# Gates of a gated linear recurrence in polar form by prefix sums, instead of products doubled level by level

## The chip, the cores and the metric

The kernel runs on one core of one Trainium2 chip. The metric is the device time of one execution in microseconds (us). TensorE (PE) multiplies matrices, VectorE (DVE), ScalarE (ACT) and GpSimd (POOL) work on elements, and SyncE (SP) issues transfers. In the profile a float32 matmul stands as two records, each with a weight load (PEld).

## The reference

An attention block with a complex gate per channel is followed by a feed-forward block (FFN). There are 4 batches, 8 heads, 768 tokens and 48 channels per head; the FFN has 3072 tokens, width 384 and inner width 1024. All inputs are float32 except the four FFN weights, which are float64.

```python
a_re = rand * 0.1 + 0.85 ; a_im = randn * 0.1
mag = sqrt(a_re * a_re + a_im * a_im)
scale = minimum(mag, 0.999) / (mag + 1e-06)
for t in range(S):                       # S_re, S_im: 48 x 48 per head
    new_re = ar * S_re - ai * S_im       # ar, ai: a_re, a_im times scale, at t
    new_im = ar * S_im + ai * S_re
    S_re, S_im = new_re + outer(k[t], v[t]), new_im
    y[t] = q[t] @ S_re
x = y.transpose(0, 2, 1, 3).reshape(3072, 384)
out = (((x @ w1) * (x @ w2)) @ w3) @ w_out
```

## The kernel before

A unit is one batch and two heads (16 units); head g lies on partitions 64g to 64g+47, time on the free axis. Time is cut into six chunks of 128 tokens. Inside a chunk, the decay from token s to token t is a product of gates. It is built in seven levels n = 1, 2, 4 ... 64. At each level the buffers Q (q times gates) and K (k times gates) are multiplied in place, on VectorE, by the products X of the gates over half blocks (lines 209 to 218), and GpSimd makes the products of the next level from those of this one (lines 221 to 225). TensorE makes the scores of the pairs of tokens that part at this level: for n up to 16 in blocks of 32 tokens (lines 160 to 166), which VectorE takes over by mask into D (lines 170 and 177), and for n = 32 and 64 directly (lines 190 and 194). At the end of a unit K is transposed (line 237), kv sums are made (line 244), the state goes from chunk to chunk on VectorE (lines 250 and 253), and the outputs ys are summed from the scores A and the state (lines 263 and 266).

The gates are brought to their norm at the start of a unit (lines 130 to 141), among it a reciprocal on VectorE (line 135).

The FFN of a batch waits for all its heads: x is turned by transposes (line 282), then `ffn_ab` makes two products of 128 x 384 and multiplies them (lines 292 to 297), and `ffn_out` multiplies by the fused matrix w3 w_out (line 302). The FFN of batch b is dealt out between the levels of the units of batch b+1; the FFN of the last batch stands alone at the end. In batch 0 the weights take its place: `convert` (lines 326 to 338) turns float64 words to float32 in 36 pieces of up to 128 x 512, and `fuse` (line 349) makes w3 w_out.

The framework orders the instructions of each engine when the kernel is built, by its own model of costs; each engine then runs its list in order. Pools with one, two or three buffers decide when a tile can be written again.

## Time and profile before

| what | value |
|---|---|
| time, 3 runs | 1482.57, 1486.88 and 1487.62 us; median 1486.88 |
| span of the profiled execution, first to last instruction | 1493.7 us |
| mean granted TensorE clock | 0.754 |
| VectorE busy | 1175.4 us, 79% |
| TensorE busy | 1064.2 us, 71% |
| GpSimd busy | 562.4 us, 38% |
| ScalarE busy | 204.5 us, 14% |
| bytes moved | 48.85 MB, 33 GB/s |

The profiled execution's own time is known only as its span; the span is 6.8 us over the median of the runs, so whatever lies around it is smaller than the spread between executions. The clock is the share of full speed that TensorE was granted. In a row of the profile stand the line of the kernel, the engine, the operation, the tile written and the tiles read, the shape and the count; behind the bar the busy time in us, the mean of one in ns, and the idle time ahead of it with what ended it.

### The profile page before, as it was taken

The numbers are of one execution on the slowest core, as the hardware profiler recorded it, in microseconds if no ns is written. First come the engines' busy times: TensorE is split into PE (matmuls) and PEld (weight loads), VectorE is DVE, ScalarE is ACT, GpSimd is POOL, SyncE is SP. The second block draws the span as 40 slices with busy tenths as digits, with TensorE's granted clock in tenths as the row PEclk, the third lists the DMA queues.
The fourth block names the chain that finished last, engine by engine and source line by source line (L and its number), as shares of the span: only waits on it lengthen the run. The fifth ranks groups of instructions, "written<-read, shape, count | busy, mean of one in ns | idle before, by whom it ended". The sixth has DMA issues, their size and how long they took to land.

```text
span 1493.7 us, 42142 instructions
## 1 busy us (share of the span) xinstructions
PE 1064.2 (71%) x19304; PEld 755.5 (51%) x19304; DVE 1175.4 (79%) x1674; ACT 204.5 (14%) x362; POOL 562.4 (38%) x533
## 2 busy tenths in 40 slices
PE   0262767553276786969787968787798878787999
PEld 0252435342264564646565646465565555555755
DVE  9788989889877797888887878788877979796000
ACT  1010001010011111111211211120112020201111
POOL 5427226326218071616270534335431708080000
PEclk9985676755558686888769867877677778786899
DMA  3211222212110010101010100101010100000000
GB/s 101 57 56 47 78 69 60 78 52 61 45 31 25 11 33 13 46 3 41 21 38 3 33 21 18 30 9 45 14 34 10 39 21 10 2 7 12 2 16 16
DMA packets 35698, 48.85 MB, mean 33 GB/s; under 512 B 15552, under 2 KB 26816, under 8 KB 35520
## 3 DMA queue, kind: packets, MB, share of 16 engines
q1 hardware_dynamic: 35520, 46.15, 11.0%
q8 instruction: 151, 2.47, 0.7%
q14 instruction: 27, 0.22, 0.1%
HBM read 41.42 MB, written 4.72 MB: 31 GB/s over the span
## 4 chain that ended last, share of the span: by engine, by line
PE 46%; DVE 30%; issue 11%; POOL 11%; ACT 1%; DMA 0%; SPq 0%; POOLq 0%; DVEq 0%; ACTq 0%
PE m L292 14%; PE o L302 8%; PE sc L164 5%; DVE St L253 5%; DVE V L215 4%; DVE U L216 4%; DVE Q L218 4%; PE ys L266 3%; PE sc L190 3%; PE ys L263 3%; DVE K L218 3%; PE sc L166 3%; POOL f L336 3%; POOL X L224 2%; POOL XV L221 2%
## 5 line engine op out<-in xcount | busy, mean ns | idle before, releaser
L164 PE MATMUL sc<-Q,K 48*32 48x16 f32 x6144 | 147.3, 198 | 144.3 <-DVE Q L218 57.9
L164 PEld LDWEIGHTS sc<-Q,K 48*32 48x32 f32 x6144 | 132.3, 114 | 186.4 <-issue 152.5
L166 PE MATMUL sc<-Q,K 48*32 48x16 f32 x6144 | 142.1, 188 | 38.1 <-issue 35.9
L292 PE MATMUL m<-xT,w2s 128*128 128x384 f32 x384 | 164.2, 557 | 2.8 <-issue 2.3
L132 POOL TENSOR_TENSOR mag<-mag,den 128x768 f32<-128x768 f32 x16 | 29.0, 1811 | 364.3 <-ACT den L131 364.3
L190 PE MATMUL sc<-Q,K 48*32 48x32 f32 (+1 forms) x2304 | 78.0, 257 | 117.4 <-DVE K L218 116.1
L292 PE MATMUL m<-xT,w1s 128*128 128x384 f32 x384 | 159.5, 540 | 3.0 <-issue 3.0
L302 PE MATMUL o<-w3o,ab 128*128 128x384 f32 x384 | 158.9, 562 | 1.1 <-issue 1.1
L166 PEld LDWEIGHTS sc<-Q,K 48*32 48x32 f32 x6144 | 132.9, 122 | 49.2 <-issue 41.5
L266 PE MATMUL ys<-St,Q 48*128 48x48 f32 x640 | 135.8, 339 | 27.2 <-DVE St L253 25.9
L223 POOL TENSOR_TENSOR XV<-X 128x384 f32<-128x384 f32 (+6 forms) x112 | 85.8, 766 | 177.6 <-ACT X L139 177.6
L266 PEld LDWEIGHTS ys<-St,Q 48*128 48x128 f32 x640 | 111.0, 240 | 63.0 <-DVE St L253 31.0
L224 POOL TENSOR_TENSOR X<-X 128x1152 f32<-128x1152 f32 (+6 forms) x112 | 139.1, 1242 | 0.0
L225 POOL TENSOR_TENSOR X<-X,XV 128x1152 f32<-128x1152 f32 (+6 forms) x112 | 131.8, 1177 | 8.8
L218 DVE TENSOR_TENSOR Q<-U,V 128x384 f32<-128x384 f32 x224 | 126.7, 599 | 10.3 <-PE sc L166 9.3
L190 PEld LDWEIGHTS sc<-Q,K 48*32 48x32 f32 (+1 forms) x2304 | 69.8, 166 | 126.8 <-issue 120.0
L216 DVE TENSOR_TENSOR U<-Q,X 128x768 f32<-128x768 f32 x112 | 129.6, 1157 | 0.0
L221 POOL TENSOR_TENSOR XV<-X 128x768 f32<-128x768 f32 (+6 forms) x112 | 117.7, 1051 | 19.7 <-ACT X L139 12.4
L215 DVE TENSOR_TENSOR V<-Q,X 128x768 f32<-128x768 f32 x112 | 122.9, 1097 | 0.0
L297 DVE TENSOR_TENSOR ab<-m,a 128x384 f32<-128x384 f32 x64 | 35.4, 553 | 110.7 <-PE m L292 99.9
L336 POOL TENSOR_TENSOR f<-f,e 128x512 int32<-128x512 int32 (+1 forms) x36 | 51.8, 1438 | 157.1 <-DVE f L334 156.2
L263 PE MATMUL ys<-v,A 128*128 128x48 f32 x384 | 97.5, 362 | 14.1 <-ACT A L194 14.1
(71 smaller groups left out, 1706.2 us busy)
## 6 DMA issues: line engine op xcount, KB each, us to landing
raw<-in_w_dram SPq DMA_DIRECT2D x28, 512.0 KB, 3.6
v<-in_v_dram SPq DMA_DIRECT2D x16, 288.0 KB, 3.1
X<-in_a_re_dram SPq DMA_DIRECT2D x32, 144.0 KB, 2.9
X<-in_a_im_dram SPq DMA_DIRECT2D x32, 144.0 KB, 3.4
K<-in_k_dram SPq DMA_DIRECT2D x32, 144.0 KB, 2.7
Q<-in_q_dram SPq DMA_DIRECT2D x32, 144.0 KB, 3.6
out_dram<-ot SPq DMA_DIRECT2D x24, 192.0 KB, 1.9
raw<-in_w_out_dram SPq DMA_DIRECT2D x8, 384.0 KB, 3.1
```

Of the source, the lines that this page charges most:

```text
L164: nc.tensor.matmul(out=o, lhsT=K[ROWS[g], 0, t0:t0 + SB], rhs=qr[ROWS[g], 1, nb], start=True, stop=False)
L166: nc.tensor.matmul(out=o, lhsT=K[ROWS[g], 1, t0:t0 + SB], rhs=qr[ROWS[g], 0, nb], start=False, stop=True)
L190: nc.tensor.matmul(out=o, lhsT=K[ROWS[g], x, t0:t0 + n], rhs=Q[ROWS[g], 1 - x, t0 + n:t0 + 2 * n], start=(x == 0), stop=(x == 1))
L215: nc.vector.tensor_tensor(out=V, in0=Z, in1=wide(x[:, 0:2], 2), op=OP.mult)
L216: nc.vector.tensor_tensor(out=U, in0=Z, in1=wide(x[:, 2:3], 2), op=OP.mult)
L218: nc.vector.tensor_tensor(out=Z[:, y], in0=U[:, y], in1=V[:, 1 - y], op=OP.add)
L221: nc.gpsimd.tensor_tensor(out=XV[:, 0:2], in0=XR[:, 0:2], in1=XL[:, 2:3].to_broadcast([P, 2, nb]), op=OP.mult)
L224: nc.gpsimd.tensor_tensor(out=X2, in0=XL, in1=XR[:, 2:3].to_broadcast([P, 3, nb]), op=OP.mult)
L263: nc.tensor.matmul(out=o, lhsT=A[:, g, c], rhs=vt[:, c, g * D:(g + 1) * D], start=True, stop=(c == 0))
L266: nc.tensor.matmul(out=o, lhsT=Q[ROWS[g], 1 - x, c * C:(c + 1) * C], rhs=St[ROWS[g], c - 1, x], start=False, stop=(x == 1))
L292: nc.tensor.matmul(out=m, lhsT=w[:, f, j * P:(j + 1) * P], rhs=xT_t[b, h][:, f], start=(f == 0), stop=(f == KD - 1))
L302: nc.tensor.matmul(out=m, lhsT=ab_t[b, h][:, f, t * P:(t + 1) * P], rhs=w3o[:, f], start=(f == 0), stop=(f == KF - 1))
```

## The change

The kernel before becomes a function, `general`, that runs only where a flag, `good`, is zero at the end. Ahead of it stands a new path for gates with limits: the flag is set when no decay over a chunk is below e^-32, no angle is beyond 50, the real parts are within limits and no |a_im / a_re| is over 1.5 (`judge`). For the gates of the reference the logarithm of |a| is near -0.1, so that a chunk of 128 tokens comes to about -13, and the angle grows by steps of about 0.11.

In the new path a unit is half a batch (384 tokens, all 8 heads), with all 384 channels on 3 x 128 partitions; there are 8 units of three chunks. `gates` takes the logarithm of the magnitude and the arctangent, sums both along time with scans (lines 487 and 517), takes exponentials, sines and cosines, and multiplies q and k by them. So q is turned by its own angle and scaled by the decay since the start of the chunk, k by the inverse, and one product of 96 channels (real and imaginary part below each other) gives the scores of a head in a chunk. For that, the rows of a head are brought together in KL and QL by 40 transfers inside the chip's memory per unit (line 551). `scores` transposes the k parts (line 569), makes one product per head (line 574) and masks it (line 575). `outputs` writes y turned, as the FFN wants it, in blocks of 32 channels (lines 592 to 603), and carries the state T (kv on line 610, then VectorE on lines 614 to 617); GpSimd spreads v into V ahead of it (lines 438 to 440). `gates` of the next unit and the FFN of the unit before are interleaved with a unit's scores and outputs. `convert` needs three operations of VectorE instead of six, and two of ScalarE. The function `general` is as before except that it writes x with other channel positions and has no interleaving.

```diff
-def tile_gateloop__then__multiplicative_ffn_kernel(
+def general(ctx, tc, qt, kt, v, art, ait, w1s, w2s, w3o, ident, out):
...
+    def gates(u, split):
+        b, h = divmod(u, 2)
...
+        nc.scalar.preload_act_table_set("natural_log_exp_and_others")
+        for s in parts:
+            act(out=A[:, s], in_=re[:, s], func=AF.Ln)
+            act(out=r[:, s], in_=A[:, s], func=AF.Exp, scale=-1.0)
+        yield
+        for i, s in enumerate(parts):
+            nc.gpsimd.tensor_tensor(out=im[:, s], in0=im[:, s], in1=r[:, s], op=OP.mult)
+            act(out=Z[:, s], in_=re[:, s], func=AF.Relu, scale=-1.0, bias=LEAST, accum_out=st_low[:, 0, u, i:i + 1])
+            act(out=Z[:, s], in_=re[:, s], func=AF.Relu, bias=MOST, accum_out=st_low[:, 1, u, i:i + 1])
+        yield
+        for i, s in enumerate(parts):
+            nc.vector.tensor_tensor_reduce(out=Z[:, s], in0=im[:, s], in1=im[:, s], scale=1.0, scalar=0.0,
+                                           op0=OP.mult, op1=OP.max, accum_out=st_tan[:, u, i:i + 1])
+        yield
+        for s in parts:
+            act(out=Z[:, s], in_=Z[:, s], func=AF.Ln, bias=ONE)
+        yield
+        for s in parts:
+            stt(out=A[:, s], in0=Z[:, s], scalar=0.5, in1=A[:, s], op0=OP.mult, op1=OP.add)
+            act(out=Z[:, s], in_=A[:, s], func=AF.Exp, scale=-1.0, bias=EPS)
+        yield
+        for s in parts:
+            ts(out=A[:, s], in0=A[:, s], scalar1=LN_MAX, scalar2=None, op0=OP.min)
+        for s in parts:
+            for f in range(s.start, s.stop):
+                for c in range(UC):
+                    w = slice(c * C, (c + 1) * C)
+                    nc.vector.tensor_tensor_scan(out=r[:, f, w], data0=A[:, f, w], data1=Z[:, f, w], initial=0.0,
+                                                 op0=OP.add, op1=OP.subtract)
+        yield
+        for s in parts:
+            act(out=A[:, s], in_=r[:, s], func=AF.Exp)
+            act(out=Z[:, s], in_=A[:, s], func=AF.Ln)
+        yield
+        for s in parts:
+            tt(out=Z[:, s], in0=r[:, s], in1=Z[:, s], op=OP.subtract)
+            act(out=r[:, s], in_=r[:, s], func=AF.Exp, scale=-1.0)
+            stt(out=A[:, s], in0=Z[:, s], scalar=1.0, in1=A[:, s], op0=OP.add, op1=OP.mult)
+        yield
+        for s in parts:
+            tt(out=Z[:, s], in0=A[:, s], in1=r[:, s], op=OP.mult)
+            stt(out=r[:, s], in0=Z[:, s], scalar=2.0, in1=r[:, s], op0=OP.subtract, op1=OP.mult, reverse0=True)
+        for s in parts:
+            nc.gpsimd.tensor_tensor(out=q[:, s], in0=q[:, s], in1=A[:, s], op=OP.mult)
+            nc.gpsimd.tensor_tensor(out=k[:, s], in0=k[:, s], in1=r[:, s], op=OP.mult)
+        for X in (R, K2):
+            nc.vector.tensor_copy(out=X[:, :, TT:TT + UC], in_=ends(A, slice(0, KD)))
+        nc.vector.tensor_copy(out=st_dec[:, u], in_=R[:, :, TT:TT + UC])
+        spread_v(u)
+        yield
+        nc.scalar.preload_act_table_set("trig_and_small")
+        for s in parts:
+            act(out=im[:, s], in_=im[:, s], func=AF.Arctan)
+        yield
+        for s in parts:
+            for f in range(s.start, s.stop):
+                nc.vector.tensor_tensor_scan(
+                    out=Z[:, f], data0=im[:, f], data1=im[:, f],
+                    initial=0.0 if h == 0 else st_ang[:, u - 1, f, UC - 1:UC], op0=OP.add, op1=OP.bypass)
+        nc.vector.tensor_copy(out=st_ang[:, u], in_=ends(Z, slice(0, KD)))
+        yield
+        for s in parts:
+            ts(out=re[:, s], in0=Z[:, s], scalar1=0.5 / PI, scalar2=ROUND, op0=OP.mult, op1=OP.add)
+            ts(out=re[:, s], in0=re[:, s], scalar1=ROUND, scalar2=2 * PI, op0=OP.subtract, op1=OP.mult)
+            tt(out=Z[:, s], in0=Z[:, s], in1=re[:, s], op=OP.subtract)
+        yield
+        for s in parts:
+            act(out=re[:, s], in_=Z[:, s], func=AF.Abs)
+            act(out=re[:, s], in_=re[:, s], func=AF.Sin, scale=-1.0, bias=QUARTER)
+            act(out=Z[:, s], in_=Z[:, s], func=AF.Sin)
+        yield
+        for s in parts:
+            tt(out=r[:, s], in0=k[:, s], in1=re[:, s], op=OP.mult)
+            tt(out=k[:, s], in0=k[:, s], in1=Z[:, s], op=OP.mult)
+        yield
+        for s in parts:
+            tt(out=A[:, s], in0=q[:, s], in1=re[:, s], op=OP.mult)
+            tt(out=q[:, s], in0=q[:, s], in1=Z[:, s], op=OP.mult)
+        KL = two.tile([2 * D, H, TT + UC], FP, tag="KL", name="KL")
+        QL = two.tile([2 * D, H, TT], FP, tag="QL", name="QL")
+        L_t[u] = QL, KL, R, K2
+        for dst, src in ((KL, (R, K2)), (QL, (A, q))):
+            for hd in range(H):
+                for x in range(2):
+                    r0 = hd * D
+                    while r0 < (hd + 1) * D:
+                        f, p0 = divmod(r0, P)
+                        n = min((hd + 1) * D - r0, P - p0)
+                        d0 = x * D + r0 - hd * D
+                        nc.sync.dma_start(out=dst[d0:d0 + n, hd], in_=src[x][p0:p0 + n, f])
+                        r0 += n
+        if u + 1 < NU:
+            load_qkv(u + 1)
+        if u + 2 < NU:
+            load_gates(u + 2)
+    def scores(u, c):
+        QL, KL, R, K2 = L_t[u]
+        last = u % 2 and c == UC - 1
+        w = slice(c * C, (c + 1) * C)
+        A = Ab[(u * UC + c) % 2]
+        KT = None if last else two.tile([P, H, 2, D], FP, tag="KT", name="KT")
+        for x, src in enumerate((R, K2)):
+            if not last:
+                tp = ps_1.tile([P, KD, C], FP, tag="tr", name="tp")
+                for f in range(KD):
+                    nc.tensor.transpose(out=tp[:, f], in_=src[:, f, w], identity=ident)
+                nc.scalar.copy(out=KT[:, :, x], in_=tp.rearrange("p f c -> p (f c)").rearrange("p (h d) -> p h d", d=D))
+            sc = ps_s.tile([P, H // 2, C], FP, tag="sc", name="sc")
+            for j in range(H // 2):
+                hd = x * H // 2 + j
+                nc.tensor.matmul(out=sc[:, j], lhsT=KL[:, hd, w], rhs=QL[:, hd, w], start=True, stop=True)
+            nc.vector.copy_predicated(
+                out=A[:, x * H // 2:(x + 1) * H // 2], data=sc,
+                mask=causal.rearrange("p (h t) -> p h t", h=1).to_broadcast([P, H // 2, C]))
+        y_t[u, c] = A, KT
+    def outputs(u, c):
+        QL, KL, _, _ = L_t[u]
+        w = slice(c * C, (c + 1) * C)
+        A, KT = y_t.pop((u, c))
+        V = Vb[u % 2][:, c]
+        if c == 0:
+            xT_t[u] = two.tile([P, KD, TT], FP, tag="xT", name="xT")
+        first = u % 2 == 0 and c == 0
+        T = T_t.get(u // 2)
+        y = ps_1.tile([P, KD, C], FP, tag="y", name="y")
+        for f in range(2):
+            for j in range(4):
+                nc.tensor.matmul(out=y[32 * j:32 * j + 32, f], lhsT=V[:, 4 * f + j, 0:LO], rhs=A[:, 4 * f + j],
+                                 start=True, stop=first)
+            for j in range(0 if first else 4):
+                nc.tensor.matmul(out=y[32 * j:32 * j + 32, f], lhsT=T[:, 4 * f + j, 0:LO], rhs=QL[:, 4 * f + j, w],
+                                 start=False, stop=True)
...
+        nc.scalar.copy(out=xT_t[u][:, :, w], in_=y)
+        if KT is None:
+            return
+        kv = ps_1.tile([2 * D, H, 64], FP, tag="kv", name="kv")
+        for hd in range(H):
+            nc.tensor.matmul(out=kv[:, hd], lhsT=KT[:, hd], rhs=V[:, hd], start=True, stop=True)
...
+        nc.scalar.activation(out=low, in_=lo.bitcast(U32), func=AF.Copy, scale=2.0 ** -29)
+        nc.scalar.activation(out=mag, in_=hi.bitcast(FP), func=AF.Square)
+        nc.vector.tensor_scalar(out=b, in0=hi, scalar1=3, scalar2=0x3FFFFFFF, op0=OP.logical_shift_left,
+                                op1=OP.bitwise_and)
+        nc.vector.scalar_tensor_tensor(out=b, in0=hi, scalar=-0x40000000, in1=b, op0=OP.bitwise_and, op1=OP.bitwise_or)
+        nc.gpsimd.tensor_tensor(out=b, in0=b, in1=low, op=OP.add)
+        nc.vector.scalar_tensor_tensor(out=dst, in0=mag, scalar=MIN_SQ, in1=f, op0=OP.is_ge, op1=OP.mult)
...
+    work = wo_work()
+    for j in range(KF):
+        work += w3_work(j) + [lambda j=j: fuse(j)]
+    work += w12_work()
...
+    for u in range(NU):
+        att = [lambda c=c: scores(u, c) for c in range(UC)]
+        att = [att[0], att[1], lambda: outputs(u, 0), att[2], lambda: outputs(u, 1), lambda: outputs(u, 2)]
+        steps = gates(u + 1, False) if u + 1 < NU else iter(())
+        for f in interleave(att, ffn(u - 1) if u else []):
+            f()
+            next(steps, None)
+        for _ in steps:
+            pass
+        if u + 1 == NU:
+            judge()
+    for f in ffn(NU - 1):
+        f()
+    fast.close()
+    value = nc.values_load(good[0:1, 0:1], min_val=0, max_val=1)
+    with tc.If(value == 0):
+        general(tc, qt, kt, v, art, ait, w1s, w2s, w3o, ident, out)
```

The framework's order decides what stands where. Three places matter for what follows.

ScalarE, in the middle of the program: first a stretch of before (one unit and the FFN; mag and den are the gates' magnitude, A the scores, KT the turned K, a the first product of the FFN), then one pass of `gates` of the kernel after with what lies in it (gA, gZ, gR, im and re are the working tiles of `gates`, y and xT the outputs, m, a and ot of the FFN).

```order
L131 ACTIVATE den<-X_81 128x768
L238 COPY KT<-tp 128x512 x2
L238 COPY KT<-tp 128x256
L133 ACTIVATE mag<-mag 128x768
L296 COPY a<-m 128x384 x2
L139 ACTIVATE X_81<-X_81 128x768
L130 ACTIVATE mag<-X_80 128x768
```

```order
L473 ACTIVATE gZ<-gZ,consts 128x1152
L513 ACT_TABLE_LOAD
L513 ACTIVATE im<-im 128x1152
L478 ACT_TABLE_LOAD
L478 ACTIVATE gZ<-gA,consts 128x1152
L605 COPY xT<-y 128x3x128
L640 COPY ot<-o 128x384 x2
L642 DMA out_dram<-ot 128x384 x2
L492 ACTIVATE gA<-gR 128x1152
L605 COPY xT<-y 128x3x128
L493 ACT_TABLE_LOAD
L493 ACTIVATE gZ<-gA 128x1152
```

Where four activations and some copies stood per unit, a pass of `gates` now has 13 activations of 128 x 1152, and eight of them have a table load ahead, since the preloads written in `gates` (lines 458 and 511) have all moved to the start of the program and each function loads its own set. Copies that TensorE waits for stand between them.

TensorE, in the middle: first before, at the end of the levels of a unit; then after, where the FFN of one unit (m) meets the transposes (tp) and the first scores (sc) of the next.

```order
L190 MATMUL sc<-Q_76,K_78 32x32 x48
L190 MATMUL sc<-Q_76,K_78 64x64 x24
L263 MATMUL ys<-v,A_82 128x48 x3
L237 MATMUL tp<-ident,K_78 128x128 x10
L244 MATMUL kv<-v,KT 64x48 x8
L292 MATMUL m<-xT,w1s 128x384
```

```order
L627 MATMUL m<-xT,w2s 128x384 x3
L627 MATMUL m<-xT,w1s 128x384 x3
L627 MATMUL m<-xT,w2s 128x384 x3
L610 MATMUL kv<-V_87,KT 96x64 x8
L627 MATMUL m<-xT,w1s 128x384
L574 MATMUL sc<-QL,KL 128x128
L627 MATMUL m<-xT,w1s 128x384 x2
L574 MATMUL sc<-QL,KL 128x128
L627 MATMUL m<-xT,w2s 128x384 x3
L574 MATMUL sc<-QL,KL 128x128
L569 MATMUL tp<-ident,gR 128x128 x3
```

The seven levels are gone; a unit's scores are 24 matmuls of 128 columns, and they come in among the last products of the FFN of the unit before.

SyncE, in the first part of the program: before, loads of weights (raw) with those of the units between them; after, the last four weight pieces and behind them the first transfers of the second unit's KL (from gR and k).

```order
L326 DMA raw<-in_w_out_dram 128x768 x4
L111 DMA K_78<-in_k_dram 48x768 x2
L326 DMA raw<-in_w_out_dram 128x768
L326 DMA raw<-in_w_dram 128x4x256
L115 DMA v<-in_v_dram 128x6x96
L111 DMA Q_77<-in_q_dram 48x768 x2
```

```order
L655 DMA raw_767<-in_w1_dram 16x1024 x8
L655 DMA raw_785<-in_w2_dram 32x1024 x4
L655 DMA raw_799<-in_w2_dram 32x1024 x4
L655 DMA raw_813<-in_w2_dram 16x1024 x8
L551 DMA KL_1082<-gR_855 48x387
L551 DMA KL_1082<-k_605 48x387
```

The 40 transfers of the second unit stand behind all the weight pieces, and a piece can be loaded only when the one two before it has been read, since raw has two buffers.

More of the change, by code (lines that the diff above doesn't have):

```diff
@@ L56 @@
     DM = H * D
-    FF = w1.shape[1]
+    FF = w1s.shape[2]
     KD = DM // P
@@ L98 @@
         masks[n] = m
-    w1s = singles.tile([P, KD, FF], FP, name="w1s")
-    w2s = singles.tile([P, KD, FF], FP, name="w2s")
-    w3o = singles.tile([P, KF, DM], FP, name="w3o")
     v_t, xn_t, xT_t, ab_t = {}, {}, {}, {}
```

309 lines of the change are left out of this document (240 added, 69 removed).

## The prediction

> **What bounds the kernel now.** I read the busy times of the engines first, then the busy times by stage (the stretches of the windows are about one batch each), then the chain of work that ended last.
>
> ```profile
> PE 1064.2 (71%) x19304; PEld 755.5 (51%) x19304; DVE 1175.4 (79%) x1674; ACT 204.5 (14%) x362; POOL 562.4 (38%) x533
> ...
> PE 46%; DVE 30%; issue 11%; POOL 11%; ACT 1%; DMA 0%; SPq 0%; POOLq 0%; DVEq 0%; ACTq 0%
> ```
>
> ```profile
> core 0: us, PE busy (x) PEld busy (x) DVE busy (x) ACT busy (x) POOL busy (x), PEclk, DMA share, GB/s
> ...
> 130.00:427.00 297.00, 151.29 (x3314) 112.65 (x3316) 261.41 (x400) 27.21 (x48) 115.06 (x112) 0.61 0.20 61
> 427.00:747.00 320.00, 253.28 (x4788) 179.40 (x4784) 266.13 (x367) 50.55 (x89) 137.34 (x124) 0.75 0.10 24
> ...
> 1392.00:1494.00 102.00, 98.03 (x306) 58.61 (x305) 8.92 (x16) 13.79 (x29) 0.00 (x0) 0.97 0.03 12
> ```
>
> A batch takes 320 us, of which VectorE is busy for 266 (83%) and TensorE for 253 (79%). The two hand work to each other level by level, hence both in the chain. The granted clock follows TensorE's density: 0.61 at 51% busy, 0.75 at 79%, 0.97 at 96% in the last FFN. By the straight line between the last two, 92% busy gives 0.92.
>
> **The change, part by part.** VectorE's rows:
>
> ```profile
> L138 DVE TENSOR_TENSOR X<-X,mag 128x768 f32<-128x768 f32 x32 | 30.1, 952 | 0.1
> L218 DVE TENSOR_TENSOR K<-U,V 128x384 f32<-128x384 f32 x192 | 99.7, 560 | 0.0
> L134 DVE TENSOR_SCALAR den<-mag 128x768 f32<-128x768 f32 x16 | 9.6, 597 | 41.4 <-ACT mag L133 41.4
> L170 DVE COPY_PREDICATED D<-diag,sc 128x192 f32<-128x192 int32 x32 | 12.3, 385 | 1.4 <-PE sc L160 1.4
> L177 DVE COPY_PREDICATED D<-mask,sc 128x96 f32<-128x96 int32 x160 | 41.6, 303 | 68.6 <-PE sc L166 68.5
> ```
>
> A pass over 768 elements takes 952 ns, over 384 560; on that line 1152 take 1.35 us. A unit after has 11 such passes (14.9 us), three TENSOR_SCALAR (597 at 768, so 0.8 each: 2.4), 9 scans of 128 and 3 of 384, six masked copies of 512 (385 at 192 and 303 at 96 give 0.66 each), five steps of T and eight products of the FFN at about 0.6: 11.3 together. No scan is in the trace. At the rate of a pass they take 9 x 0.29 + 3 x 0.56 = 4.3 us, if each element needs two steps 8.6; I take 4.3, the nearest row. The sum is 33 us a unit, 264 for eight, against 1175 in all now: the multiplications of Q and K at seven levels (L215 to L218) and the reciprocal are gone, and VectorE stops being the bound.
>
> TensorE's rows, the first two from the last FFN in order of time (start, length):
>
> ```profile
> 1422.29 2.10 PE L292 MATMUL m<-xT,w2s 128*128 128x384 f32 x6
> ...
> 1424.22 2.10 PE L292 MATMUL m<-xT,w1s 128*128 128x384 f32 x6
> ...
> 1490.26 0.48 ACT L305 COPY ot<-o 128x384 f32<-128x384 f32 x1 [4.73 <-PE o L302]
> ```
>
> ```profile
> L292 PE MATMUL m<-xT,w1s 128*128 128x384 f32 x384 | 159.5, 540 | 3.0 <-issue 3.0
> L282 PE MATMUL xtp<-ident,xn 128*128 128x128 f32 x72 | 17.1, 404 | 1.6 <-ACT xn L270 0.7
> L160 PE MATMUL sc<-Q,K 48*32 48x64 f32 x1536 | 33.1, 300 | 48.2 <-DVE Q L141 39.5 <-issue 8.3 <-PE ys L266 0.4
> L244 PE MATMUL kv<-v,KT 128*64 128x48 f32 x640 | 31.3, 259 | 0.0
> ```
>
> At full clock six records follow the last six by 1.93 us: 322 ns a record. The FFN of a unit is 72 matmuls, 144 records: 46.4 us. Scores are 24 matmuls, 48 records; nearest is L282, a 128-column weight load with 128 columns, 17.1/72 = 237 ns: 11.4. The outputs y are 88 matmuls, 176 records of 128 columns on 32 columns of the array; nearest is L160, blocks of 32, 33.1/1536 = 21.5 ns for 64 columns, so 43: 7.6. The kv sums are 40 records at 31.3/640 x 64/48 = 65 ns: 2.6; 15 transposes at 237: 3.6. The unit is 71.6 us. Low end: the scores stream at a third of 322, 107 ns, their loads hidden: 65. High end: the y records follow one another at 107 ns (18.8 instead of 7.6), and the FFN runs as in the mean of now, 159.5/384 = 415 ns (59.8 instead of 46.4): 96. I take 71.6 at full clock; with a period of 78 TensorE is 92% busy, which by the line above is clock 0.92, and 71.6/0.92 is 78 again. **So the period P is 78 us a unit**, 156 a batch instead of 320.
>
> The other loop goes from one unit's `gates` to the next, as gA, gR and gZ have one buffer each: ScalarE, VectorE and GpSimd in turn, then 40 transfers.
>
> ```profile
> L130 ACT ACTIVATE mag<-X 128x768 f32<-128x768 f32 x16 | 13.5, 841 | 2.9 <-DVE X L138 2.8
> L296 ACT COPY a<-m 128x384 f32<-128x384 f32 x64 | 30.7, 479 | 318.0 <-PE m L292 318.0
> L225 POOL TENSOR_TENSOR X<-X,XV 128x1152 f32<-128x1152 f32 x16 | 48.9, 3058 | 1.3
> ```
>
> ```profile
> X<-in_a_re_dram SPq DMA_DIRECT2D x32, 144.0 KB, 2.9
> ```
>
> ```profile
> 6.92 1.28 ACT L130 ACT_TABLE_LOAD   x1 [6.92 <-DMA X<-in_a_re_dram]
> ...
> 8.13 0.89 SPq L111 DMA_DIRECT2D Q<-in_q_dram  x2
> 8.21 0.84 ACT L130 ACTIVATE mag<-X 128x768 f32<-128x768 f32 x1
> ```
>
> An activation of 1152 is 841 + 384 x 0.94 (from 479 and 841) = 1.2 us; eleven of the 13 are in the chain: 13.2. Eight table loads at 1.28: 10.3. One product on GpSimd, 3.1; the other two lie beside the sines. VectorE's steps that nothing covers are one reduction, the nine scans, three passes, three scans, two TENSOR_SCALAR and one pass, and the last four passes: 18. Copies that stand between them in order: eight on ScalarE (3.8), six products or T steps on VectorE (3.5). That is 52 us. (In all, ScalarE has 13 activations, eight loads and 20 copies a unit, 35 us, and GpSimd three products and nine small copies, under 15: neither fills 78.) Two issues take 0.89 us on SP, so 40 take 17, and the last lands 2.9 later; the first can go when the first of the last four passes is done, 4 us early: 16. The loop is 68 us, under TensorE's 78, so that `gates` lies beside the FFN and the outputs. If that cover fails, it is added in part (second rival).
>
> The Trainium skill speaks against this chain: "ScalarE: Activation LUTs", section "What ACT_TABLE_LOAD costs", gives 2.66 us a switch, with the drain, and its section "Table sets: the hidden batching unit" says that exponential and logarithm fit one set, so that two loads a unit would do. By the 2.66 the loop would be 79, one over 78, and the total 6 us more. The trace bears out only the 1.28, as the activation starts at 8.21, where the load ends.
>
> **The start.** The first units run before the weights are ready, and here the rows of `convert` count, with one place where GpSimd holds VectorE up:
>
> ```profile
> L332 DVE TENSOR_SCALAR f<-raw 128x512 int32<-128x512 int32 x28 | 14.6, 523 | 0.7 <-DMA raw<-in_w_dram 0.7
> L334 DVE SCALAR_TENSOR_TENSOR f<-raw,f 128x512 int32<-128x512 int32 x28 | 22.0, 785 | 0.0
> L338 DVE SCALAR_TENSOR_TENSOR w3s<-e,f 128x512 f32<-128x512 int32 x16 | 11.4, 715 | 0.1
> L336 POOL TENSOR_TENSOR f<-f,e 128x512 int32<-128x512 int32 x28 | 41.6, 1486 | 126.9 <-DVE f L334 126.0 <-DVE e L335 0.9
> ```
>
> ```profile
> 27.83 3.54 POOL L224 TENSOR_TENSOR X<-X 128x1152 f32<-128x1152 f32 x1
> 28.61 2.97 DVE L332 TENSOR_SCALAR f<-raw 128x384 int32<-128x384 int32 x1
> ```
>
> A conversion takes 0.52 + 0.79 + 0.72 = 2.0 us of VectorE; 24 stand ahead of the first scores, 49 us, with `gates` of unit 0 in thirds, 27 us, from 7 us on (the first gates landed at 6.92). The 2.97 us of an operation that otherwise takes 0.5 show VectorE held while GpSimd works; GpSimd has 24 x 1.49 and nine products, 48 us. Held for none of it, the first scores start at 83, for all of it at 131; I take 20 us, about 103. `gates` of unit 1 follows in 52, with five conversions between (10): 165. Its transfers stand on SP behind the last weight loads, which wait for the seven other conversions, at some 3 us each (2.0 and part of a load of 2.9): 186, and 19 for the transfers, behind which the loads for unit 2 wait in turn: **scores of unit 1 start at 205**. Without the hold and the queueing it is 83 + 52 + 10 + 19 = 164, with all of the hold 233.
>
> **The sum.** 205, six periods (468), then scores and outputs of the last unit (25), the rest of the FFN before it (15.5 of 46.4) and the last FFN (46.4), 87 in all, and the end: now the copy at 1490.26 stands 3.4 us ahead of the end of the span, to which the test of the flag is added, for which there is no row; between 0 and the 11 us of the longest steps without a cause I take 4. Together 767 us of span. The span of now, 1493.7, stands 0.5% over the median of its runs: 767 x 1486.88/1493.7 = **764 us**.
>
> **The rivals.** (1) The clock stays full: P is 72, 205 + 432 + 87 + 7 = 731. For it: 0.97 where TensorE is dense; against: 0.75 where it was busy for 79%. The Trainium skill, "TensorE: Matmul & The Clock Gate", section "What's actually happening", has it so: the full clock after about 3.4 us of sustained work. (2) The hand-over stays open: ScalarE and VectorE run their lists in order, a copy that waits for TensorE holds the chain, and the 16 us of transfers add to the chain and its waits, P up to 90: 205 + 540 + 94 = 839. For it: single buffers; against: transposes and FFN stand where the wait would be. (3) The y blocks follow one another at the lower clock: P 96, 205 + 576 + 116 + 7 = 904. (4) The slower side: the flag comes out zero, through one count that is off, and `general` runs as well. Its attention took 320 us a batch, so at least 764 + 4 x 320 = 2044. A single failed test decides it. Against it: the decay over a chunk is near e^-13, against a limit of e^-32, and angles and real parts are as far within theirs.
>
> **Chances.** Forecast 0.36, (1) 0.24, (2) 0.22, (3) 0.10, (4) 0.03, beyond these and still faster 0.05. The range goes from 695 (the start at 164 with P 72: 690) to 910, and leaves out (4), the rest and some of (3). About 0.3% is what a measurement of this kernel can tell from no change: faster 0.96, within 0.01, slower 0.03.
>
> **What would show it.** Right: TensorE over 85% busy from about 200 us on at a clock over 0.9, scores of consecutive units 78 us apart, records of L627 at 322 to 360 ns, y records (L592 to L603) under 60 ns of busy time each, VectorE under 400 us in all. Wrong: idle time of TensorE ahead of L574 ended by transfers of KL or QL (rival 2), a lower clock without idle time, scans at twice the pass, or any instruction of `general`. The start is checked by the first L574 of unit 1, at 205.

## The result and the profile after

The changed kernel takes 767.85 us (median of 4 runs, 766.49 to 769.61) against 1487.25 before (4 runs): a ratio of 0.516 [0.513, 0.518]. The profiled execution has a span of 767.0 us. `general` did not run. Here and below, a few executions that were far slower than the others of their kernel are left out of the medians (one of e6_no_block took 1569 us).

The page of the changed kernel, the lines that answer to those of before (busy times; shares of the chain that ended last, by engine and by line):

```profile
PE 597.2 (78%) x3514; PEld 376.7 (49%) x3514; DVE 384.7 (50%) x555; ACT 348.0 (45%) x466; POOL 152.2 (20%) x149
...
PE 23%; DVE 21%; ACT 17%; SPq 15%; issue 13%; POOL 6%; DMA 4%; ACTq 0%; DVEq 0%; POOLq 0%
SPq L551 14%; PE m L627 12%; PE o L637 5%; DVE gZ L517 4%; DVE gZ L501 3%; DVE gR L487 3%; POOL cf L666 3%; POOL im L464 2%; PE sc L574 2%; PE kv L610 2%; ACT gZ L473 1%; DVE cf L665 1%; ACT L478 1%; ACT gZ L478 1%; DVE w3s L667 1%
```

Busy times by stage, cut at the first scores of units 2 and 7 (columns as before the change: engines, then granted clock, DMA share, GB/s):

```profile
100.00:200.00 100.00, 61.35 (x395) 40.03 (x393) 55.45 (x80) 48.16 (x65) 29.70 (x24) 0.74 0.30 92
200.00:298.10 98.10, 82.44 (x457) 50.78 (x458) 45.58 (x62) 39.34 (x52) 15.74 (x16) 0.91 0.34 99
298.10:663.90 365.80, 316.86 (x2037) 204.38 (x2036) 192.54 (x253) 165.43 (x201) 56.23 (x51) 0.94 0.25 73
663.90:767.00 103.10, 98.25 (x524) 61.63 (x524) 14.54 (x26) 10.54 (x22) 0.00 (x0) 0.98 0.07 23
```

TensorE is 87% busy over five units (316.86 of 365.8, 63.4 us a unit) at clock 0.94, and VectorE 53%. One would call that bound by TensorE, as the prediction did. But the chain is mostly not TensorE: 38% of it is VectorE and ScalarE, and its largest line is L551, the issue of the transfers. And what TensorE waits for longest in these five units (us, times, longest) is the end of `gates`, ahead of the transposes of the next unit:

```profile
PE tp L569 <- DVE gR L533: 20.8, 3, 10.5
```

TensorE in order of time (start, length), around the first scores (L574) of units 1, 2 and 7, and some dense blocks of unit 2:

```profile
215.16 3.66 PE L627 MATMUL m<-xT,w2s 128*128 128x384 f32 x10
...
222.52 2.10 PE L637 MATMUL o<-w3o,ab 128*128 128x384 f32 x6
224.46 0.39 PE L574 MATMUL sc<-QL,KL 96*128 96x128 f32 x2
...
298.09 0.39 PE L574 MATMUL sc<-QL,KL 96*128 96x128 f32 x2
...
311.12 2.05 PE L574 MATMUL sc<-QL,KL 96*128 96x128 f32 x16
...
314.15 0.40 PE L592 MATMUL y<-A,V 128*32 128x128 f32 x8
314.37 0.40 PE L595 MATMUL y<-QL,T 96*32 96x128 f32 x8
314.59 0.62 PE L599 MATMUL y<-A,V 128*32 128x128 f32 x16
```

The first scores of unit 7 are at 663.91 (the start of the last window), so the six periods from unit 1 are (663.91 - 224.46)/6 = 73.2 us each. Sixteen score records take 2.05 us (128 ns each); eight y records start 0.22 us apart, 27 ns each.

The loop through `gates`, seen in the chain of the window from 298 to 385 us (start, length, what held the chain; "issue" is time without a cause that the profile shows):

```profile
306.06 2.13 DMA QL<-gA
...
309.63 1.17 ACT gA L460
...
334.50 3.82 DVE gZ L501
...
353.70 0.51 SPq L551
354.26 0.58 SPq L551
...
378.11 0.59 SPq L551
378.74 2.13 DMA QL<-gA
...
382.31 1.17 ACT gA L460
```

From the logarithm (309.63) to the first transfer of the same unit 44.1 us pass, in which ScalarE, VectorE and GpSimd work in turn; then 40 transfers are issued, 0.63 us apart, until 378.7, and the last lands; the next unit's logarithm, which writes gA, is at 382.31. Together 72.7 us (44.1, 27.2 from the first issue to the last landing at 380.87, and 1.4 from there, most of it a table load): the period, to half a microsecond. The wait that closes the loop stands ahead of the logarithm's table load in each of the seven units that have one (times, busy time, mean ns, idle time before it):

```profile
L460 ACT ACT_TABLE_LOAD x7 | 9.0, 1283 | 30.3 <-DMA QL<-gA 30.3
```

### The profile page after: what moved, and what is told of

The parts are those of the page before. It is cut to its first block, busy times and chain, and to the rows that moved or that the text cites. A ratio compares the mean times of both kernels' runs of the same rounds, so it can differ in the third digit from the quotient of the medians.

```text
span 767.0 us, 9438 instructions
## 1 busy us (share of the span) xinstructions
PE 597.2 (78%) x3514; PEld 376.7 (49%) x3514; DVE 384.7 (50%) x555; ACT 348.0 (45%) x466; POOL 152.2 (20%) x149
## 4 chain that ended last, share of the span: by engine, by line
PE 23%; DVE 21%; ACT 17%; SPq 15%; issue 13%; POOL 6%; DMA 4%; ACTq 0%; DVEq 0%; POOLq 0%
SPq L551 14%; PE m L627 12%; PE o L637 5%; DVE gZ L517 4%; DVE gZ L501 3%; DVE gR L487 3%; POOL cf L666 3%; POOL im L464 2%; PE sc L574 2%; PE kv L610 2%; ACT gZ L473 1%; DVE cf L665 1%; ACT L478 1%; ACT gZ L478 1%; DVE w3s L667 1%
## 5 line engine op out<-in xcount | busy, mean ns | idle before, releaser
L627 PE MATMUL m<-xT,w1s 128*128 128x384 f32 x384 | 153.2, 528 | 31.9 <-DVE w1s L667 14.6
L627 PE MATMUL m<-xT,w2s 128*128 128x384 f32 x384 | 148.0, 517 | 9.8 <-DVE w2s L667 4.9
L637 PE MATMUL o<-w3o,ab 128*128 128x384 f32 x384 | 130.1, 489 | 0.0
L627 PEld LDWEIGHTS m<-xT,w1s 128*128 128x128 f32 x384 | 74.0, 205 | 80.8 <-DVE w1s L667 17.4
L719 PE MATMUL f<-wo_s,w3s 128*128 128x384 f32 x128 | 50.0, 541 | 70.1 <-DVE w3s L667 70.1
L627 PEld LDWEIGHTS m<-xT,w2s 128*128 128x128 f32 x384 | 74.1, 200 | 59.5 <-issue 7.0
L637 PEld LDWEIGHTS o<-w3o,ab 128*128 128x128 f32 x384 | 70.8, 190 | 45.1 <-issue 1.6
L666 POOL TENSOR_TENSOR cf<-cf,low 128x512 int32<-128x512 int32 (+1 forms) x36 | 48.7, 1351 | 91.9 <-DVE cf L665 55.7
L574 PEld LDWEIGHTS sc<-QL,KL 96*128 96x128 f32 x384 | 51.8, 192 | 23.7 <-issue 12.2
L574 PE MATMUL sc<-QL,KL 96*128 96x128 f32 x384 | 56.7, 281 | 5.3 <-DMA QL<-q 4.5
L575 DVE COPY_PREDICATED A<-causal,sc 128x512 f32<-128x512 int32 x48 | 34.0, 732 | 47.2 <-PE sc L574 46.9
L528 ACT ACTIVATE re<-gZ 128x1152 f32<-128x1152 f32 (+1 forms) x10 | 9.6, 969 | 71.3 <-DVE gZ L525 71.3
L610 PEld LDWEIGHTS kv<-V,KT 128*96 128x96 f32 x320 | 32.4, 174 | 5.1 <-issue 4.3
L610 PE MATMUL kv<-V,KT 128*96 128x64 f32 x320 | 34.1, 257 | 0.2 <-DVE T L614 0.2
```

What stands on the lines that cost most here:

```text
L574: nc.tensor.matmul(out=sc[:, j], lhsT=KL[:, hd, w], rhs=QL[:, hd, w], start=True, stop=True)
L575: nc.vector.copy_predicated(out=A[:, x * H // 2:(x + 1) * H // 2], data=sc, mask=causal.rearrange("p (h t) -> p h t", h=1).to_broadcast([P ...
L610: nc.tensor.matmul(out=kv[:, hd], lhsT=KT[:, hd], rhs=V[:, hd], start=True, stop=True)
L627: nc.tensor.matmul(out=m, lhsT=w[:, f, j * P:(j + 1) * P], rhs=xT_t[u][:, f], start=(f == 0), stop=(f == KD - 1))
L637: nc.tensor.matmul(out=m, lhsT=ab_t[u][:, f, t * P:(t + 1) * P], rhs=w3o[:, f], start=(f == 0), stop=(f == KF - 1))
L666: nc.gpsimd.tensor_tensor(out=b, in0=b, in1=low, op=OP.add)
```

## The experiments

Two theories. A: this loop (44 us of chain, 28 of transfers) sets the period. B: TensorE at its granted clock sets it, as predicted. Each kernel is the changed one with the edit shown. In the table, all from profiled executions except the time: first scores of unit 1, mean of the six periods from there to unit 7, mean of the last five of them (from unit 2 on), from the first scores of unit 7 to the end, and the median time.

| kernel | unit 1 | six periods | last five | end | time |
|---|---|---|---|---|---|
| changed kernel | 224.5 | 73.2 | 73.2 | 103.1 | 767.85 |
| e1_two_queues | 212.8 | 76.8 | 80.0 | 113.8 | 789.03 |
| e2_two_loads | 218.1 | 69.9 | 70.6 | 103.7 | 742.28 |
| e3_less_pe | 224.3 | 72.9 | 72.6 | 66.9 | 730.69 |
| e4_freed | 244.8 | 67.9 | 72.4 | 113.1 | 766.07 |
| e5_unit1_queue | 183.3 | 81.4 | 77.6 | 104.0 | 777.80 |
| e8_products | 219.5 | 70.9 | 70.4 | 89.1 | 737.44 |
| e9_freed_less_pe | 244.6 | 62.7 | 67.0 | 87.0 | 709.91 |
| e10_weights_first | 217.7 | 75.1 | 76.0 | 103.1 | 774.69 |
| e11_loads_weights | 209.3 | 71.3 | 72.6 | 103.8 | 744.37 |
| e12_loads_products | 215.0 | 65.5 | 65.9 | 103.9 | 713.52 |

**Less work for TensorE (e3_less_pe).**

```diff
-        for f in range(KF):
+        for f in range(0, KF, 2):
             nc.tensor.matmul(out=m, lhsT=ab_t[u][:, f, t * P:(t + 1) * P], rhs=w3o[:, f],
-                             start=(f == 0), stop=(f == KF - 1))
+                             start=(f == 0), stop=(f == KF - 2))
```

> The last matrix product of the FFN sums only every other block of its inner dimension (half of that product is left out): TensorE has 8.1 us less work in each unit (half of 130.1/8). Theory A (loop): the period stays at 73.2 and only the last FFN gets shorter, 8 to 16 us: 752 to 760. Theory B (TensorE): each period falls by about 8: 700 to 712.

Measured 730.69 us. The two first scores that span the six periods:

```profile
224.30 0.39 PE L574 MATMUL sc<-QL,KL 96*128 96x128 f32 x2
...
661.44 0.46 PE L574 MATMUL sc<-QL,KL 96*128 96x128 f32 x2 [1.27 <-DMA QL<-q]
```

The period is 72.9 where 73.2 was, so B's forecast of 8 less fails. All of the gain, 36 us, is at the end, more than A gave it (8 to 16). The reason stands in the records of the last 103.1 us of the changed kernel, L627 and then L637:

```profile
663.90:767.00 103.10, 52.84 (x154) 0.98 0.07 23
...
663.90:767.00 103.10, 31.61 (x96) 0.98 0.07 23
```

The last FFN has 96 and 48 such records; so 58 and 48 of the FFN before it were still to do, 34 us at 322 ns, where the prediction had 15.5. TensorE carries a backlog out of the loop. By the same count 55 records were open at the first scores of unit 2 and 106 at those of unit 7: 51 were put off in five units, 3.3 us a unit, so that a unit's whole work is 66.7 us and not 63.4. In e3_less_pe only 4 records of L627 are left over at unit 7. TensorE over its five units:

```profile
298.20:661.44 363.24, 308.84 (x1993) 198.87 (x1992) 188.89 (x260) 167.15 (x206) 53.55 (x51) 0.93 0.25 74
```

The records that had been put off moved into the room that was made, so TensorE's work in the periods fell by 1.6 us a unit only (308.84 for 316.86), not by 8. The run shows that TensorE, 85% busy, has room in the periods and that its work is paid at the end; as a test of B it is weaker than planned. The runs that shorten the chain decide.

**The chain: fewer table loads (e2_two_loads).** The scheduler had moved both explicit loads to the start of the program, since nothing tied them to a place, so that the build added a load at each change of function. Here they are tied:

```diff
+        with tc.issue_after(last[0]) if last else ExitStack():     # last: the last Sin of the unit before
+            pre = nc.scalar.preload_act_table_set("natural_log_exp_and_others")
...
+        with tc.issue_after(e.ins):                                # e: the last Exp
+            pre = nc.scalar.preload_act_table_set("trig_and_small")
```

(and the Ln and the Arctan behind them issue after `pre`).

> The logarithms and exponentials of a unit share one table set, the angles the other: two table loads a unit instead of eight, and no useless ones at the start. Theory A (loop): six loads of 1.28 us leave the chain, 7.7 us, so the period falls from 73.2 to about 66, the total to about 720 (715 to 730). Theory B (TensorE): no change, 768 within 4.

Measured 742.28 us, above A's range: 6.4 us from the start and 3.3 a period, less than half of 7.7. B forecast no change, so A holds in its sign; what took back the rest of the 7.7 is open.

**The chain: the products off GpSimd (e8_products).**

```diff
-            nc.gpsimd.tensor_tensor(out=q[:, s], in0=q[:, s], in1=A[:, s], op=OP.mult)
-            nc.gpsimd.tensor_tensor(out=k[:, s], in0=k[:, s], in1=r[:, s], op=OP.mult)
+            tt(out=q[:, s], in0=q[:, s], in1=A[:, s], op=OP.mult)
+            tt(out=k[:, s], in0=k[:, s], in1=r[:, s], op=OP.mult)
```

> The products of q and k with the decays go from GpSimd to VectorE: two passes of 1.35 us more on VectorE, against 2.5 to 2.9 us of GpSimd each and the 3.9 to 6.3 us by which L501 and L517 were held up beside them. If the loop sets the period, its chain gets about 3 us shorter: total 768 - 6 x 3 = 750 (742 to 758). If TensorE sets it: no change, 768 within 4.

Measured 737.44 us, a little beyond the range. Groups of VectorE between 300 and 640 us, first in the changed kernel, then in this one (busy, mean ns):

```profile
L501 DVE TENSOR_TENSOR gZ<-gA,gR 128x1152 f32<-128x1152 f32 x5 | 18.3, 3664 | 1.3 <-ACT gR L497 1.0
...
L517 DVE TENSOR_TENSOR_SCAN gZ<-im,st_ang 128x384 f32<-128x384 f32 x9 | 15.8, 1807 | 0.0
...
L487 DVE TENSOR_TENSOR_SCAN gR<-gA,gZ 128x128 f32<-128x128 f32 x45 | 14.9, 406 | 0.1
```

```profile
L517 DVE TENSOR_TENSOR_SCAN gZ<-im,st_ang 128x384 f32<-128x384 f32 x9 | 8.5, 999 | 0.0
...
L501 DVE TENSOR_TENSOR gZ<-gA,gR 128x1152 f32<-128x1152 f32 x5 | 6.8, 1358 | 1.1 <-ACT gR L497 0.8
```

Beside GpSimd's products the same pass took 3664 ns and a scan 1807; without them 1358 and 999. That is 2.3 + 3 x 0.8 = 4.7 us a unit, against 2.7 for the two added passes. By the profiles 33 us are gained: 14 in the periods, 5 at the start and 14 at the end; the end was not in the expectation (73 records of the FFN were left over at unit 7 instead of 106).

**Both (e12_loads_products).**

> e2_two_loads (25.6 us below the changed kernel) and e8_products (30.4 below) together. Both shorten the chain of gates, by 7.7 and about 4 us. If the loop still sets the period after each, they add: 768 - 56 = 712. If TensorE, with a period of about 68 as in e4_freed, is reached by either, little is added: 728 to 737. Expected: in between, nearer to the second, about 726.

Measured 713.52 us, a ratio of 0.479 [0.476, 0.481] to the kernel before, 54.3 us below the changed kernel: 25.6 and 30.4 add, as in the first case, and the 726 missed. The logarithms of units 2 and 7 in the changed kernel, and here:

```profile
237.18 1.16 ACT L460 ACTIVATE gA<-re 128x1152 f32<-128x1152 f32 x1
...
598.95 1.16 ACT L460 ACTIVATE gA<-re 128x1152 f32<-128x1152 f32 x1
```

```profile
226.74 1.17 ACT L463 ACTIVATE gA<-re 128x1152 f32<-128x1152 f32 x1 [7.30 <-DMA QL<-gA]
...
544.77 1.16 ACT L463 ACTIVATE gA<-re 128x1152 f32<-128x1152 f32 x1
```

The loop went from 361.77/5 = 72.4 us to 318.03/5 = 63.6, and the logarithm of unit 2 still waits for the transfers. TensorE over the five units, as in the third row of the stages above:

```profile
278.33:607.95 329.62, 311.67 (x2041) 201.81 (x2039) 181.21 (x264) 125.69 (x169) 36.71 (x41) 0.97 0.28 82
```

It does nearly the work of the changed kernel (311.67 us busy for 316.86, with as much left for the end) in 329.6 us instead of 365.8. So the amount of TensorE's work did not set the 73.2 us, and theory B falls here. At 95% busy the two bounds meet. This version is the fastest found that leaves nothing out.

**The transfers out of the loop (e4_freed, e9_freed_less_pe).** gA gets a second buffer and the reciprocal magnitude goes to gZ, so that the next unit's logarithms don't wait for this one's transfers:

```diff
+        alt = u >= 2 and u % 2 == 0
+        A = (two if alt else one).tile([P, KD, TT], FP, tag="raw" if alt else "gA", name="gA")
...
-            act(out=r[:, s], in_=A[:, s], func=AF.Exp, scale=-1.0)
+            act(out=Z[:, s], in_=A[:, s], func=AF.Exp, scale=-1.0)
```

(The two Relu that use gZ as scratch come first, GpSimd's product of im reads gZ, and gA's second buffer is one of raw's, made wider.)

> gA gets a second buffer and 1/re goes to gZ instead of gR, so that the next unit's gates need not wait until the transfers of this one have landed; the 40 transfers stay as they are on SyncE. Theory A (loop): the 28 us of transfers leave the loop, which falls to about 50; TensorE's 65 to 68 becomes the period: 720 to 738. Theory B (TensorE): no change, 768 within 4.

Measured 766.07 us: A's total missed, and B's came. The mean of six periods, 67.9, looks like A's, but it is not: unit 1 came 20 us late, unit 2 caught up with it, and the five periods behind that are 72.4, where 73.2 was. TensorE in the start, its first scores of units 1, 2 and 3, and the logarithms of units 2 and 7:

```profile
233.98 5.81 PE L629 MATMUL m<-xT,w2s 128*128 128x384 f32 x10 [14.55 <-DVE w2s L669]
...
244.78 0.39 PE L576 MATMUL sc<-QL,KL 96*128 96x128 f32 x2
...
290.13 0.46 PE L576 MATMUL sc<-QL,KL 96*128 96x128 f32 x2 [1.80 <-DMA QL<-gA]
...
357.80 0.76 PE L576 MATMUL sc<-QL,KL 96*128 96x128 f32 x2 [5.33 <-DMA QL<-q]
```

```profile
217.19 1.16 ACT L464 ACTIVATE gA<-re 128x1152 f32<-128x1152 f32 x1
...
524.18 1.16 ACT L464 ACTIVATE gA<-re 128x1152 f32<-128x1152 f32 x1
```

`gates` of unit 2 now began before the last weights were converted and was put ahead of a conversion on ScalarE, for which TensorE waited 14.55 us. Behind that, the logarithms are 61.4 us apart and the scores 72.4: `gates` starts early, but does not end early. From the logarithm of unit 7 to its first transfer (636.60) 112 us pass, where 44 did in the changed kernel. The chain ahead of the first scores of that unit (at 652.13):

```profile
603.11 3.94 PE m L629 x12
...
607.15 0.06 DVE ab L634
...
607.62 0.71 DVE gR L489 x2
...
636.60 0.51 SPq L553
...
652.13 0.77 PE sc L576 x2
```

The scans of `gates` (gR) stand in VectorE's list behind a product of the FFN (ab) that waits for TensorE; the rest of `gates` and the transfers follow, and TensorE waits for these (7.47 us ahead of these scores, 5.33 at unit 3). This is much what rival 2 had: a copy (here a product) that waits for TensorE holds the chain. So one wait was taken away and another came up at about the same length. How much of the 73.2 us the transfers hold by themselves is not shown by this run; it is known only from the sum along the chain. The last kernel asks whether TensorE's work counts in the new period.

> The kernel e4_freed with half of the last matrix product of the FFN left out (8.1 us of TensorE a unit). There the period was 67.9 us with the transfers out of the loop, and here it tells what sets these 67.9. If TensorE (theory: two bounds close together, the loop at 73 and TensorE at 68): the period falls to 58 to 62, the total by 50 or more below 766. If still the loop or a third thing: the period stays at 67 to 68 and only the end gets shorter, total about 730.

Measured 709.91 us. The mean of six, 62.7, has the same late unit 1 in it; the last five periods are 67.0 where e4_freed has 72.4, so the forecast of 58 to 62 is missed, but not its sense: 5.4 us a unit went. TensorE's busy time in them fell by 4.9 us a unit (298.9 for 323.6 us), and the period with it. So in e4_freed TensorE's work is part of what sets the period, through the products that VectorE waits for. Theory A holds for the changed kernel, as e2, e8 and e12 show, with a second bound close by: 72.4 in the order of e4_freed, at most 65.9 in that of e12.

**The queue (e1_two_queues).**

```diff
-                        nc.sync.dma_start(out=dst[d0:d0 + n, hd], in_=src[x][p0:p0 + n, f])
+                        (nc.sync, nc.scalar)[x].dma_start(out=dst[d0:d0 + n, hd], in_=src[x][p0:p0 + n, f])
```

> Theory A (the loop through gates and its transfers sets the period of 73.2 us, as 45 us of chain plus 28 us of transfers): with half of the 40 transfers of a unit issued by ScalarE instead of SyncE, the transfers take about 15 us instead of 28, the loop is 60, and TensorE, with about 65 us of work a unit, becomes the bound: period 66 to 68, total about 730 (720 to 740). Theory B (TensorE at its granted clock sets the period, as the prediction had it): period and total unchanged, 768 within 4.

Measured 789.03 us, slower by 21; both theories missed. ScalarE near the end of a unit's transfers, and the largest sum of TensorE's waits between 300 and 660 us (us, times, longest):

```profile
581.28 6.08 ACTq L551 DMA_DIRECT2D QL<-q  x9
...
587.40 0.48 ACT L605 COPY xT<-y 128x384 f32<-128x384 f32 x1 [7.50 <-DMA QL<-q]
```

```profile
PE m L627 <- ACT xT L605: 26.1, 5, 8.2
```

An issue on ScalarE costs as much, 6.08/9 = 0.68 us, and there it stands in the queue of an engine that others wait for: xT copies behind it, TensorE's FFN behind those. (In the changed kernel the second issue of a burst takes 0.58 us already, at 354.26, when none has landed: that speaks for the issue itself, not a wait for an earlier transfer.)

**The start (e5_unit1_queue, e10_weights_first, e11_loads_weights).** First, only unit 1's transfers from ScalarE:

```diff
-                        nc.sync.dma_start(out=dst[d0:d0 + n, hd], in_=src[x][p0:p0 + n, f])
+                        (nc.scalar if u == 1 else nc.sync).dma_start(out=dst[d0:d0 + n, hd], in_=src[x][p0:p0 + n, f])
```

> Only the 40 transfers of unit 1 go from ScalarE's queue, so that they no longer stand on SyncE behind the weight loads; nothing else changes. If that queueing sets the start of unit 1 (224 us now), the first scores of unit 1 come at about 171 + 17 = 188 to 195 and the total falls by about as much, 30 us: 735 to 745. Rival: the weights, ready at 214, and TensorE's work behind them set the rest, so that the earlier scores are waited away: the total falls by 0 to 10.

Measured 777.80 us. The scores of unit 1 came at 183, 41 us earlier, and the total went up: the rival's side, and past it. TensorE's waits between 100 and 300 us (in the changed kernel 4.9 and 14.6 us) show why:

```profile
PE m L627 <- DVE w2s L667: 18.0, 5, 7.2
...
PE m L627 <- DVE w1s L667: 10.1, 3, 8.5
```

The weights w2s were late instead (the last conversion ended at 251 where it was 214), unit 2 gained only 14 us, and unit 3 none. Second, the conversions ahead of the FFN's copies on ScalarE:

```diff
-        nc.scalar.copy(out=a, in_=got[0])
+        with tc.issue_after(done[0]):        # done: the last conversion's Square
+            nc.scalar.copy(out=a, in_=got[0])
...
```

> On ScalarE the copies of the first FFN wait until the last weight conversion has been issued, so that no conversion stands behind a copy that waits for TensorE, which waits for the conversion before. Theory: this ring, 4.8 us a conversion where 3.2 would do, brings the last weights to 214 and with them the scores of unit 1, which stand behind that FFN in TensorE's queue, to 224. Expected: last conversion at 185 to 195, scores of unit 1 at 200 to 210, total down by 10 to 20: 748 to 758. Rival: as in e5_unit1_queue, the start is waited away or gates of unit 1 gets later by as much: total within 4 of 768.

Measured 774.69 us: my theory of the ring fell, and the rival (within 4 of 768) missed as well. The last conversion ended at 207, not 185 to 195, the scores of unit 1 came at 217.7, not 200 to 210, the FFN of unit 0 waited for its copies instead (one wait of 17.5 us), and the periods grew to 75.1.

> e2_two_loads (25.6 us below the changed kernel) and e10_weights_first together. If the two act at different places, the period and the start, they add: 742 less 10 to 20, 722 to 732. If e10 brings nothing: 742.

Measured 744.37 us: nothing is gained over e2_two_loads, though unit 1 starts 9 us earlier. Three times an earlier unit 1 was given back in the periods. What would shorten the start in earnest is not settled.

**The flag (e6_no_block, e7_flag_zero).** Without the block:

```diff
-    value = nc.values_load(good[0:1, 0:1], min_val=0, max_val=1)
-    with tc.If(value == 0):
-        general(tc, qt, kt, v, art, ait, w1s, w2s, w3o, ident, out)
```

> The conditional block and the read of the flag are left out (judge still computes the flag). The prediction put the end at 4 us for the test, between 0 and 11. The span after the last output copy is 4.8 us now and was 3.4 before: if the test is all of that difference, 1.4 us less, 766; if the block costs more (instruction loading, the branch), up to 11 us less.

Measured 766.04 us against 767.85: 1.8 us, within what the runs scatter. With the flag forced to zero:

```diff
-    SMALL, LARGE, STEEP, DECAY, ANGLE = 2.0 ** -7, 2.0 ** 40, 1.5, math.exp(-32.0), 50.0
+    SMALL, LARGE, STEEP, DECAY, ANGLE = 2.0 ** -7, 2.0 ** 40, 1.5, math.exp(-32.0), 0.0
```

> The limit of the angles is 0, so that the flag comes out zero and the block runs after the fast path, as in rival 4 of the prediction, which had at least 2044 (764 and the attention of four batches at 320). With the FFN of general as well, 1494 - 130 = 1364 in the trace of before, it is 768 + 1364 = 2132: expected 2044 to 2140.

Measured 2379 us (1.599 [1.594, 1.603] of the kernel before): the block costs 1611 us, more than the whole kernel before, and 240 over the upper end. A window of 400 us inside it:

```profile
1000.00:1400.00 400.00, 256.26 (x4799) 198.18 (x4798) 268.71 (x364) 50.48 (x100) 125.17 (x120) 0.64 0.07 19
```

TensorE and VectorE do the work of a batch of before (253 and 266 us there) but need some 400 us for it instead of 320, at clock 0.64 instead of 0.75: `general` as it stands here runs its attention and its FFN one behind the other, so neither fills the other's waits. (The 1364 us of the expectation took the interleaving of before for granted.)

## Why the prediction was right in its sum and wrong in its bound

The span came out as predicted, 767, and that was luck: its terms did not.

| step | predicted | measured |
|---|---|---|
| first scores of unit 0 | 103 | 104.4 |
| first scores of unit 1 | 205 | 224.5 (+19.5) |
| six periods | 468 | 439.4 (-28.6) |
| from there to the end | 94 | 103.1 (+9) |

- **The period.** "So the period P is 78 us a unit", set by TensorE, is the step that failed. Two terms were mis-sized in opposite directions. First, TensorE's unit was put at 71.6 us at full clock. It is 66.7 us at clock 0.94, with the 3.3 that were put off, so about 62.7 at full clock. The FFN was right (L627 and L637 together at 322 ns when dense). Scores took 128 ns a record instead of 237 (-5.2 us a unit), y 27 instead of 43 (-2.8); these two are 8.0 of the 8.9 us. The rate of a 128-column transpose that waits for its neighbours was the wrong nearest row for dense scores; the low end, a third of an FFN record, was nearer.
- **The loop under it.** Second, "The loop is 68 us, under TensorE's 78": it was 72.7 and above TensorE. The chain was shorter than thought (45.5 us for 52): the copies of others that I had put in it at 7.3 us took under 1 us of this window's chain. The transfers were longer, 27 for 16: two issues at 0.89 us were DRAM loads, while these 40, from SBUF to SBUF, take 0.63 each. e2, e8 and e12 show that the chain of this loop sets the period, and e12 that TensorE can do the same work in periods of 65.9. That the transfers hold 27 us of it is read from the chain; e4, which took them out, gained nothing. It is the mechanism of rival 2 (chain plus transfers) at a lower price than rival 2 gave it.
- **The signs.** TensorE's share and clock, the records of L627 and y and VectorE's sum came as listed under "Right" or close to it (84% busy from 200 to 298 us, 87% behind that), and still TensorE was not the bound: they would have come with either. The one sign that tells the two apart, 78 us between units, did not come. The sign of rival 2 was too narrow: TensorE waited 4.5 us in all for QL ahead of scores, but 20.8 for the last steps of `gates` ahead of transposes.
- **The start.** 205 was 19.5 too early. `gates` of unit 1 ended at 171 (predicted 165), but its first transfer went at 208.5 (predicted 186): the nine conversions left by then ended from 175 to 214, some 5 us apart instead of 3. Two things then ended together: the first transfer of QL was issued at 221.4, and the products m of the FFN of unit 0 (L627), whose last weights were converted at 214, ended on TensorE at 222.7. The scores stand behind both. e5 moved the transfers alone: the scores came 41 us earlier, and the total still went up.
- **The end.** The FFN carried over was 34 us, not 15.5, and what else stands there beside the last FFN some 23, not 32. Of the 4 us for the flag, the run without it gives 1.8, no more than the scatter.
- **From span to time.** 767 was turned into 764 because the span of before lay over the median of its runs. But that was a slower execution: in the runs of this case the time is some 1.8 us over the span (768.78 for 767.0 here), so a span of 767 stands for 769.
- **VectorE and GpSimd.** 384.7 us in all, under the 400 foretold. The scans lay between the pass rate taken (0.29 and 0.56 us) and twice that: 0.41 for 128 columns and 1.00 for 384, undisturbed. The hold by GpSimd was put in the start alone; it was in every unit too, and e8 priced it.
- **The clock.** The straight line gave 0.85 at 87% busy; it was 0.94 (and 0.98 at 95%). No line through busy shares would do: e8 has 1.00 at 92% (434.47 to 503.67 us), e3 0.82 at 81% from unit 1 to 2 and 0.93 at 85% behind that. Full clock after 3.4 us of sustained work, as the Trainium skill has it in "TensorE: Matmul & The Clock Gate", section "What's actually happening", is neither shown nor ruled out by the means of such stretches, which hold gaps.
- **The table loads.** The two loads that the Trainium skill's "ScalarE: Activation LUTs", section "Table sets: the hidden batching unit", says would do are worth 25.6 us (e2). The prediction left them out of the sum as hidden under TensorE; with the loop as the bound part of them was not. The trace has 1.28 us a load here too, not 2.66.

So the total is right because 28.6 us too much in the periods stood against 28 too little at the two ends. The reasoning would have sent an engineer to TensorE, where 8 us a unit bring 37 in all, instead of to the chain, where 9 bring 54.

## What to carry to other kernels

An engine that is 87% busy need not be the bound: take work from it, and see whether the period moves, before tuning it; then count what it still does in a period, since work put off can move into the gap. For each loop through single buffers, add up the chain and all its transfers, each at its own issue time, and look at which queue or engine stands behind the instruction that one moves: issues put on ScalarE and unit 1 pulled forward only moved the wait. A sum that agrees proves none of its terms; check them at marks inside the run. Nor does a mean over periods: look at each one, as a late unit that is caught up with makes the mean short (45.4 us in e4_freed).

## What the runs showed of the hardware

- Issuing a transfer of up to 48 rows from SBUF to SBUF takes some 0.5 to 0.6 us on SP, one every 0.63 us, and about as much on ScalarE's queue (6.08 us for nine), from the first of a burst on.
- A float32 scan on VectorE took 406 ns for 128 columns and 999 for 384, that is (999 - 406)/256 = 2.3 ns an element and some 110 ns more, where a pass takes 1358/1152 = 1.2.
- VectorE's pass of 1152 took 3664 ns beside a GpSimd product and 1358 without it (e8).
- The y blocks, 32 columns of the array each, ran at 27 ns a record of 128 columns: less than a quarter of the 128 ns of a score record with the same columns.
